# Two layers of spectral mixing and attention: later row aggregation, one product for the values, query halves, middle rows turned by DMA, a new order

## The chip, the cores and the metric

The kernel runs on one core of a Trainium2 chip. The metric is the device time of one execution in microseconds, lower is better. A core has five engines that run their own instruction queues in order and meet at semaphores: TensorE (PE in the profile, with its weight loads as PEld), VectorE (DVE), ScalarE (ACT), GpSimd (POOL) and SyncE (SP), which here only issues DMAs.

## The reference

The input x has 2048 rows of 512 bf16 values. Two pairs of layers follow each other. A mixing layer takes the layer norm of x, its two-dimensional real Fourier transform, multiplies it with a complex weight, transforms back and adds the result to x. An attention layer takes the layer norm of x, makes 32 query heads of 16 columns each with one shared key and value head, and adds the projected result.

```python
def _layernorm(x, axis=-1, eps=1e-5):
    m = jnp.mean(x, axis=axis, keepdims=True)
    v = jnp.var(x, axis=axis, keepdims=True)
    return (x - m) / jnp.sqrt(v + eps)
...
def _A_ref(x, w_r, w_i):
    X = rfft2(x.astype(jnp.float32))
    X = X * (w_r + 1j * w_i)
    return irfft2(X, s=(S, D)).astype(jnp.bfloat16)
...
q, k, v = heads(x @ wq), x @ wk, x @ wv
scores = jnp.einsum("bhqd,bkd->bhqk", q, k) * (Dh ** -0.5)
p = _softmax(scores, axis=-1)
o = jnp.einsum("bhqk,bkd->bhqd", p, v)
return merged(o) @ wo
...
x = x + _A_ref(_layernorm(x), A_w_r, A_w_i)
x = x + _B_ref(_layernorm(x), B_wq, B_wk, B_wv, B_wo)
x = x + _A_ref(_layernorm(x), A_w_r, A_w_i)
x = x + _B_ref(_layernorm(x), B_wq, B_wk, B_wv, B_wo)
```

## The kernel before

The rows stay in on-chip memory as `x_sb`, in four tiles t = 0 to 3 of four row groups r = 0 to 3 with 128 rows each. A layer (a mixing and an attention, class `Layer`) has these stages.

*Front* (`add_stats`, `add_front`). For each tile, VectorE takes `bn_stats` and `bn_aggr` of each row group (`bn`), ScalarE makes the reciprocal deviation with a logarithm and an exponential (`rstd`, which adds the epsilon from a small tensor `eps`), TensorE turns pairs of row groups (`tr_x`) and multiplies them with the Fourier table (`mm1`), ScalarE scales the result (`mm1_evac`), and VectorE combines the four row groups (`radix_g`). In layer 2 the first three tiles are turned by DMA instead: `turn_x` writes a pair of row groups to a DRAM buffer `way` and a DMA transpose reads it back (`turned`).

*Middle* (`add_middle`). TensorE transforms along the rows (`mid`, L1207 to L1209), ScalarE copies, VectorE multiplies with the weight (`filt`, L1233 to L1236).

*Back* (`add_back`). For each tile t the inverse transform (`inv`, L1262), its copies, the radix step on VectorE (`radix_v`), the last product (`y_mm`, L1306), and the sum with x: for t = 0 on TensorE and a ScalarE copy (`put_x`, L1313), otherwise on VectorE (`add_x`, L1317). Then the second layer norm: `bn` (L1091, L1092), `rstd` (L1103, L1104), `shift` (L1108, the negated product of mean and reciprocal deviation) and `apply` (L1115). TensorE turns the normalised rows (`tr_n`, L1323), VectorE or ScalarE copies them (`trn_evac`, L1326), and TensorE makes the keys (`k_mm`, L1340), queries and values (`v_mm`, L1352). `k_evac` (L1346, L1348) writes the keys of even and odd heads to `KA` and `KB`; `v_evac` (L1360, L1362) writes four copies of the values, each with its own factor, since VectorE's approximate exponential is a sum of three phases.

*Attention* (`Attn`). There are 32 blocks: four groups of 512 query rows (qb), four groups of eight heads (g) and two parities of heads (par, which picks `KA` or `KB`). A block has 64 units of 128 keys by 512 queries of one head. A unit goes one of two ways. ScalarE takes two units at once through its exponential (`exp`, L1387). VectorE takes one unit through a multiply-add to 16-bit integers (`p1`, L1394), and two more phases of four units follow, on GpSimd (`phase`, L1398) or VectorE (L1400). TensorE makes the scores (`scores`, L1382) and accumulates the products with the values (`pv`, L1404). When a block is done, `evac` (L1411) transposes it in blocks of 32; after two parities `recip` (L1416), `mul` (L1422) and a turn follow, by DMA (`norm_dma`) or for the last two blocks on VectorE (`norm`, L1431); after four g, `close_rows` projects the rows (`proj`, L1447) and adds them to x. In layer 1 this starts the next layer's front for those rows; in layer 2 each row group is written out (L1453).

The order of all instructions is made ahead of time by a planner (class `Plan`). It keeps a clock for each engine, prices each task, and at each step issues the task that can start first. Background tasks have a priority, an order number and a delay (`lazy`). For a DMA turn it expects a fixed time: `TURN` is 7000 ns and `OUT_TURN` 25000 ns. `fill` puts products of zeros (`dummy`, L1073) into TensorE's queue where it would be idle, which keeps its clock up. VectorE takes units only once the values of all four tiles are there (`dve_on`). A string `SCRIPT` lists steps at which the planner's choice is to be changed: a number of steps, and a kind of change from `TURNS`. `RANKS` is empty and has no effect.

The planner's scores use two PSUM tiles of two banks for ScalarE (`sa`) and four single banks (`b`), which VectorE's scores share with the accumulators and all background products.

Of the kernel before, what the change touches and what calls it, by code (L numbers as in the profile page):

```python
# [10 lines left out]
P = 128  # L11
# [8 lines left out]
R = 4  # L20
# [69 lines left out]
def phase_weights():  # L90
# [4 lines left out]
RANKS = ((), ())  # L95
TURNS = ("PE", "ACT", "DVE", "POOL", "wait", "few", "heads", "phase")
SCRIPT = (
    "0ax00902q00k05h0hw0po0c807l04j03c00801i00a00p0740ay04w00p01v0vn01903p0790l900i01f0630fk00q01202z0ad09i01h07k0h8"
    "08t0ib00a02g04s0bp08300c02q05k05101200q02300s00903n0960b202107m0ac07h00e00e01e0dc03g0by04r0500bx0rl00g0q803f06u"
    "03d03s02t00a01c08001401711p01q05g00j0ex0iy00t01a03807p05t08200k07409503o00g00x00g03914a00804107x04k01m0310ix00s"  # L100
    "02400u0rv02g05707s09a08805q02o03u02206s0mg03l01k02o03u01t00c04w07401m01l01o09s0d90w50ak0240ng09e03407500p00w00c"
    "06o06d08t03h02l0650c81380aq04o04u01h03f00r08i0190dc0bh11p0ud0e404z02103c01l01n02502s05k09906903f01y00x016018083"
    "03h00y02w02l01x06j0hy00o00r0at01q00z00w05n06m0lt05e00c05k0fx0i00740200m40560fx0mh01i00h04402000d00x02j07102x00k"
    "0b201101l0fc04t06q00p01101y0ls00m04w00i05n01x00j00902803m00s03m02u00l01808y0ba0a50z80wa00s0hw08o02c0ml084")


def script():

    out, n = {}, 0
    for i in range(0, len(SCRIPT), 3):  # L110
        v = int(SCRIPT[i:i + 3], 36)
        n += v // 8
        out.setdefault(n, []).append(TURNS[v % 8])
    return out


class Task:
# [5 lines left out]
    def __init__(self, eng, dur, deps, fn, take=None, give=(), then=None, prio=-1, order=0, lazy=0.0, gap=0.0, parts=1, port=False, lock=False, cols=None):  # L123
# [7 lines left out]
        self.end = self.slot = None  # L131


class Plan:
# [34 lines left out]
    OUT_TURN = 25000.0  # L169
# [3 lines left out]
    def __init__(self):  # L173
        self.t = {"PE": 0.0, "ACT": 0.0, "DVE": 0.0, "POOL": 0.0}
# [18 lines left out]
        self.ranks, self.base = None, 0  # L193

    def ranked(self, which):

        self.ranks, self.base = RANKS[which], self.n

    def add(self, *a, **kw):
        k = Task(*a, **kw)  # L200
        k.seq, k.born = self.n, self.t[k.eng]
        self.n += 1
        if self.ranks is not None and k.order < 30:
            i = k.seq - self.base
            if i < len(self.ranks):
                k.prio, k.order, k.lazy = -1, self.ranks[i] / 32, 0.0
        for e in k.ways:
            self.bg[e].append(k)
        return k
# [14 lines left out]
    def step(self):  # L224
        while True:
# [13 lines left out]
            self.turns.discard(eng)  # L239
            return  # L240
# [36 lines left out]
    def bg_next(self, eng):  # L277
        best = None
        for k in self.bg[eng]:
            if any(d.end is None for d in k.deps):  # L280
                continue
            if eng == "ACT" and len(k.ways) > 1 and self.at is not None and self.at.dve_on:
                continue
# [106 lines left out]
    def usable(self, kind):  # L390
# [9 lines left out]
        else:  # L400
            sd, free = (sum(1 for x in self.use if x == y) for y in ("sd", None))
            if not free or sd >= 3 or not at.dve_on and (sd >= self.EARLY_SD or free < 2 or not at.begun or us[0][1] // 4 not in at.v_ready):
                return False
# [3 lines left out]
        return at.unit_ready(us[0]) is not None  # L407

# [87 lines left out]
    def fill(self, start, after):  # L496
# [3 lines left out]
        while self.activity(start) < warm:  # L500
# [8 lines left out]
            else:  # L509
                return  # L510
            if start - t0 < self.MM + (self.PE_SW if mode != after else 0.0) and self.activity(start) >= force:
                return
# [3 lines left out]
            self.t["PE"] = t0 + self.MM  # L516
            if fresh:
                self.bank[i] = t0 + self.MM
# [115 lines left out]
class Attn:  # L634


    def __init__(self, plan, em, layer):
        self.plan, self.em, self.layer = plan, em, layer
        self.blocks = [(qb, g, par) for qb in range(NQB) for g in range(4) for par in range(2)]
        nb = len(self.blocks)  # L640
        first = [(b, 4 * t + r) for t in range(4) for b in range(layer.NFIRST) for r in range(4)]
# [53 lines left out]
    def unit_ready(self, u):  # L695
        b, kc, h = u
        qb, g, par = self.blocks[b]
        if (g, qb) not in self.qt_ready or (kc // 4, par) not in self.k_ready:
            return None
        return max(self.qt_ready[(g, qb)], self.k_ready[(kc // 4, par)])  # L700
# [10 lines left out]
    def done(self, b, slot, end):  # L711
# [5 lines left out]
        self.evac[b] = self.evac_last = ev  # L717
        if par == 0:
            return
        tail = 0.0 if b >= len(self.blocks) - 2 else 5000.0  # L720
        rc = p.add("DVE", 260.0, [ev, self.evac[b - 1]], lambda k: em.recip(self, b), lazy=tail)
        mu = p.add("DVE", 600.0, [rc], lambda k: em.mul(self, b), lazy=tail, port=True)
        if b < len(self.blocks) - 2:
            no = Mark("DMA", None)

            def turned(k):
                em.norm_dma(self, b)
                no.end = k.end + p.OUT_TURN

            mu.then = turned  # L730
        else:
            no = p.add("DVE", 626.0, [mu], lambda k: em.norm(self, b), lazy=tail)
        self.evac[b] = no
        if g == 3:
            self.layer.close_rows(qb, [self.evac[8 * qb + 2 * i + 1] for i in range(4)])


class Layer:
# [9 lines left out]
    PUTC = True  # L748
    FIRST_PUT = (0,)
    BN = ((4,), (4,), (4,), (2, 2))  # L750
    FIRST_EV = ("ACT",)
    FIRST_EV2 = ("ACT",)

    def __init__(self, plan, em, first, last):
# [5 lines left out]
        self.mm1_done = {}  # L760
        self.g_done = {}
# [5 lines left out]
    def pieces(self, durs, deps, fn, order, lazy=0.0, lock=False):  # L767

        for i, d in enumerate(durs):
            deps = [self.plan.add("DVE", d, deps, lambda k, i=i: fn(i), order=order, lazy=lazy, port=True, lock=lock)]  # L770
        return deps[0]


    def add_stats(self, key, tiles, deps):
# [3 lines left out]
        for i, (t, r) in enumerate(tiles):  # L778
            y = getattr(deps[i], "put", None)
            ks.append(p.add("DVE", 795.0, deps[i:i + 1], lambda k, i=i, y=y: em.bn(self, key, i, tiles[i], len(tiles), y and y.slot),  # L780
                            lazy=0.0 if y else 3000.0, order=5))
            if y:
                deps[i].x = p.add("ACT", 482.0, deps[i:i + 1], lambda k, t=t, r=r, y=y: em.put_x(t, r, y.slot), order=1)
                p.both(deps[i].x, ks[-1], y)
        self.add_rstd(key, tiles, ks)

    def add_rstd(self, key, tiles, ks):
        k = self.plan.add("ACT", 450.0, ks, lambda k: self.em.rstd(self, key, len(tiles)), order=5)
# [73 lines left out]
    def add_back(self):  # L862
        p, em, at = self.plan, self.em, self.at
        left = [T]
        for t in range(T):
            o = 20 + 10 * t
            cs = []
            for b in range(2):
# [17 lines left out]
                cs.append(self.pieces((332.0, 332.0, 400.0, 400.0), es, lambda i, t=t, b=b: em.radix_v(self, t, b, i), o))  # L886
            w = 2 if t == 0 else R
            te = []
            for j in range(0, R, w):
                key, ks = ("b", t, j), []  # L890
                for i, r in enumerate(range(j, j + w)):
                    put = t in self.FIRST_PUT
                    n = 5 if put else 4
                    y = p.add("PE", 217.0 * n, cs, lambda k, s, t=t, r=r, n=n: em.y_mm(self, t, r, k.slot, s, n), parts=n, take="b",
                              order=o + 1)
                    if put:
                        c = p.add("ACT", 482.0, [y], lambda k, t=t, r=r, y=y: em.put_x(t, r, y.slot), order=o + 1)
                        b = p.add("DVE", 795.0, [y], lambda k, key=key, i=i, t=t, r=r, w=w, y=y:
                                  em.bn(self, key, i, (t, r), w, y.slot), order=o + 2)
                        p.both(c, b, y)  # L900
# [3 lines left out]
                    ks.append(p.add("DVE", 795.0, [z], lambda k, key=key, i=i, t=t, r=r, w=w: em.bn(self, key, i, (t, r), w),  # L904
                                    order=o + 2))
                rs = p.add("ACT", 450.0, ks, lambda k, key=key, w=w: em.rstd(self, key, w), order=o + 3)
                nb = p.add("DVE", 100.0, [rs], lambda k, key=key, w=w: em.shift(self, key, w), order=o + 3)
                for i, r in enumerate(range(j, j + w)):
                    self.stat[("b", t, r)] = (rs, key, i)
                for a in range(j, j + w, 2):  # L910
                    ap = [p.add("DVE", 323.0, [nb], lambda k, t=t, r=r: em.apply(self, t, r), order=o + 3) for r in (a, a + 1)]
# [24 lines left out]
            p.add("DVE", 524.0, [m], lambda k, t=t, m=m: em.v_evac(t, m.slot), give=(m,), then=v_got, order=o + 6)  # L936
# [5 lines left out]
    def close_rows(self, qb, deps):  # L942
# [595 lines left out]
```

The softmax here doesn't subtract the row's maximum and nothing guards it: scores larger than these inputs give would overflow.

## Time and profile before

| | |
|---|---|
| time, median of 3 runs | 1314.85 us (1314.13 to 1315.22) |
| span of the profiled execution | 1312.7 us |
| granted TensorE clock | 1.00 |
| DMA | 33.04 MB, mean 25 GB/s |

Each stage has its place in the span. Layer 1's front lies before about 23 us, its middle between 22 and 50 us, its back between 50 and 108 us, and its attention runs until 666 us. Layer 2's last tile goes through the front until 682 us, its middle until about 706 us, its back until 760 us, and its attention until 1304 us; the last rows are written after that. In the page's second part each digit is the busy tenth of one of 40 slices of the span:

```profile
DVE  6999999999999999999979999999999999999998
ACT  6488999999999999999954899999999999999996
```

VectorE and ScalarE are full in both attentions; the low digits of ScalarE are the front, middle and back stages of the two layers.

A line of the timeline has the start in us, the duration in us, the engine, the line of the code, the operation, output and inputs, and in brackets the idle time before it with what ended it. Durations overlap a little where an engine starts an instruction before the one ahead has ended, so the step from start to start is the cost.

### The profile page before, as it was taken

What the parts mean: (1) busy time and instruction counts of PE and PEld (TensorE: products, weight loads), DVE (VectorE), ACT (ScalarE), POOL (GpSimd) and SP (SyncE); (2) the same over time, 40 slices, a digit from 0 to 9 for tenths busy, and PEclk for the clock granted to TensorE, in tenths of its full rate; (3) what the DMA queues carried; (4) which work ended last, traced back from release to release, by engine and by line L of the source; (5) the groups of instructions that cost most, each with busy time, mean ns of one, the idle gap of its engine ahead of it and who ended that gap; (6) DMA issues with size and microseconds to landing.
All of it is one profiled execution on the core that took longest, in us unless ns stands there. A gap on an engine that the chain in (4) does not pass through costs nothing.

```text
span 1312.7 us, 31767 instructions
## 1 busy us (share of the span) xinstructions
PE 1281.5 (98%) x12986; PEld 433.1 (33%) x12986; DVE 1272.7 (97%) x2277; ACT 1223.3 (93%) x1397; POOL 840.1 (64%) x825
## 2 busy tenths in 40 slices
PE   9999999999999999999999999999999999999997
PEld 5642222322232222222256423232222232233222
DVE  6999999999999999999979999999999999999998
ACT  6488999999999999999954899999999999999996
POOL 0005777767777677766720067787777777777775
PEclk9999999999999999999999999999999999999999
DMA  9100000011010100010051000000100010000101
GB/s 294 46 1 1 10 9 10 9 32 19 2 12 12 36 10 10 9 34 17 10 169 41 1 1 9 10 10 9 22 14 10 9 22 14 5 8 11 27 5 25
DMA packets 108722, 33.04 MB, mean 25 GB/s; under 512 B 88352, under 2 KB 107296, under 8 KB 108576
## 3 DMA queue, kind: packets, MB, share of 16 engines
q1 hardware_dynamic: 108288, 30.46, 10.0%
q8 instruction: 101, 1.65, 0.5%
q10 hardware_dynamic: 288, 0.56, 0.1%
q14 instruction: 45, 0.37, 0.1%
HBM read 17.89 MB, written 7.60 MB: 19 GB/s over the span
## 4 chain that ended last, share of the span: by engine, by line
ACT 72%; PE 18%; DVE 10%; issue 1%; DVEq 0%
ACT e_0_84 L1387 3%; ACT e_10_94 L1387 3%; ACT e_13_97 L1387 3%; ACT e_3_87 L1387 3%; ACT e_20_104 L1387 3%; ACT e_4_88 L1387 3%; ACT e_12_96 L1387 3%; ACT e_2_86 L1387 3%; ACT e_8_92 L1387 3%; ACT e_7_91 L1387 3%; ACT e_11_95 L1387 3%; ACT e_18_102 L1387 3%; ACT e_1_85 L1387 3%; ACT e_5_89 L1387 3%; ACT e_15_99 L1387 3%; ACT e_14_98 L1387 3%
## 5 line engine op out<-in xcount | busy, mean ns | idle before, releaser
L1382 PEld LDWEIGHTS <-KB 32*128 32x128 bf16 x2048 | 89.7, 91 | 228.5 <-issue 221.4
L1382 PEld LDWEIGHTS <-KA 32*128 32x128 bf16 x2048 | 86.4, 91 | 238.4 <-issue 231.5
L1404 PEld LDWEIGHTS <-vs_116 128*32 128x32 bf16 x2474 | 99.9, 94 | 93.0 <-issue 87.9
L1404 PEld LDWEIGHTS <-vs_117 128*32 128x32 bf16 x1622 | 96.0, 94 | 64.0 <-issue 60.5
L1404 PEld LDWEIGHTS <-vs_118 128*32 128x32 bf16 x1622 | 70.6, 94 | 70.5 <-issue 65.9
L1404 PEld LDWEIGHTS <-vs_119 128*32 128x32 bf16 x1622 | 68.4, 94 | 64.8 <-issue 61.4
L1398 POOL INT64_ADD w_1382<-w_1381 x1 | 1.0, 1040 | 108.1 <-DVE w_1381 L1394 108.1
L1398 POOL INT64_ADD w_10977<-w_10976 x1 | 1.0, 1038 | 97.2 <-DVE w_10976 L1394 97.2
L1387 ACT ACTIVATE e_6_90<-sa_64 128x1024 bf16<-128x1024 f32 x34 | 39.8, 1172 | 1.0 <-PE sa_65 L1382 1.0
L1091 DVE BATCH_NORM_STATS2 st<-x_sb 128x6 f32<-128x512 bf16 x52 | 35.4, 682 | 4.0 <-DMA x_sb<-in_A_x_dram 3.6
L1387 ACT ACTIVATE e_11_95<-sa_65 128x1024 bf16<-128x1024 f32 x31 | 36.5, 1178 | 0.7 <-PE sa_65 L1382 0.7
L1387 ACT ACTIVATE e_12_96<-sa_65 128x1024 bf16<-128x1024 f32 x31 | 36.9, 1189 | 0.2 <-PE sa_65 L1382 0.2
L1387 ACT ACTIVATE e_2_86<-sa_64 128x1024 bf16<-128x1024 f32 x31 | 36.5, 1178 | 0.4 <-PE sa_64 L1382 0.4
L1387 ACT ACTIVATE e_4_88<-sa_65 128x1024 bf16<-128x1024 f32 x31 | 36.6, 1182 | 0.1
L1387 ACT ACTIVATE e_1_85<-sa_64 128x1024 bf16<-128x1024 f32 x31 | 36.6, 1180 | 0.1
L1387 ACT ACTIVATE e_7_91<-sa_64 128x1024 bf16<-128x1024 f32 x31 | 36.6, 1181 | 0.0
L1387 ACT ACTIVATE e_15_99<-sa_65 128x1024 bf16<-128x1024 f32 x31 | 36.6, 1179 | 0.0
L1387 ACT ACTIVATE e_20_104<-sa_65 128x1024 bf16<-128x1024 f32 x31 | 36.4, 1175 | 0.0
L1387 ACT ACTIVATE e_13_97<-sa_64 128x1024 bf16<-128x1024 f32 x31 | 36.2, 1168 | 0.0
L1387 ACT ACTIVATE e_14_98<-sa_65 128x1024 bf16<-128x1024 f32 x31 | 36.0, 1162 | 0.0
L1387 ACT ACTIVATE e_0_84<-sa_65 128x1024 bf16<-128x1024 f32 x30 | 35.5, 1183 | 0.2 <-PE sa_65 L1382 0.2
L1387 ACT ACTIVATE e_9_93<-sa_64 128x1024 bf16<-128x1024 f32 x30 | 35.1, 1170 | 0.2 <-PE sa_64 L1382 0.2
(4077 smaller groups left out, 6474.8 us busy)
## 6 DMA issues: line engine op xcount, KB each, us to landing
it<-const_IT SPq DMA_DIRECT2D x8, 640.0 KB, 5.6
onw<-on SPq DMA_DIRECT2D x120, 32.0 KB, 1.9
x_sb<-in_A_x_dram SPq DMA_DIRECT2D x4, 512.0 KB, 6.8
out_dram<-x_sb SPq DMA_DIRECT2D x16, 128.0 KB, 1.9
way<-x_sb SPq DMA_DIRECT2D x6, 256.0 KB, 2.2
tab_PH<-const_PH ACTq DMA_DIRECT2D x1, 512.0 KB, 4.9
w_131<-const_FT SPq DMA_DIRECT2D x1, 512.0 KB, 8.8
w_136<-const_FT SPq DMA_DIRECT2D x1, 512.0 KB, 8.4
```

The lines of the kernel that those rows point to most:

```text
L1091: self.nc.vector.bn_stats(st, self.ps(slot) if slot else self.x[:, x[1], x[0], :])
L1382: self.nc.tensor.matmul(o, lhsT=KX[rs, kc * P:(kc + 1) * P], rhs=at.QT[qb][rs, g, :], start=True, stop=True, skip_group_check=True)
L1387: self.wrote("ACT", e, self.nc.scalar.activation(out=e, in_=self.ps(slot), func=ACT.Exp, scale=SCALE))
L1398: self.nc.gpsimd.int64_add(t[p][:, 0:n].bitcast(U64), t[0][:, 0:n].bitcast(U64), DELTA[p] * FOUR)
L1404: self.nc.tensor.matmul(self.ps(slot)[32 * h:32 * h + 32, :], lhsT=V[:, kc, :], rhs=rhs, start=first, stop=last, skip_group_check=True)
```

## The change

The parts are these.

- `bn` aggregates a row group's statistics when those of the next one have been taken; the last call of a group aggregates what is left. The planner's price goes from 795 ns each to 585, 685 or 800 ns.
- `rstd` takes the epsilon as an immediate number. `shift` is gone: `apply` subtracts the mean and multiplies by the reciprocal deviation.
- `v_evac` writes all four value copies with one VectorE product; the factors stand in a small tensor `vw` that GpSimd fills.
- The normalised rows of tiles 1 and 2 are turned by DMA (`turn_n`: two writes of one row group each and a transpose of both), not by TensorE and a copy.
- In the back, `y_mm` of a row group waits only for the radix piece that makes it, and row groups go in the order 0, 2, 1, 3 for tiles 0 and 3.
- The last two blocks of a layer (`halves`) no longer take one parity of heads with 512 queries but both parities with 256 queries each. Each of their scores is two products of 256 columns. `recip`, `mul`, `norm` and `close_rows` follow after each of them, for two row groups.
- The first tile of x is loaded in two halves, arrival times and the price of zero products before 4400 ns are changed, `OUT_TURN` is 9000 ns.
- `TURNS` has a ninth kind, `flex` (ScalarE may take a copy that VectorE could take too, also during full attention); VectorE's scores leave a bank free when an urgent product of `close_rows` needs it; `SCRIPT` is new.

```diff
-TURNS = ("PE", "ACT", "DVE", "POOL", "wait", "few", "heads", "phase")
+TURNS = ("PE", "ACT", "DVE", "POOL", "wait", "few", "heads", "phase", "flex")
...
-    OUT_TURN = 25000.0
+    COLD = 4400.0
+    OUT_TURN = 9000.0
...
-        self.t = {"PE": 0.0, "ACT": 0.0, "DVE": 0.0, "POOL": 0.0}
+        self.t = {"PE": 1200.0, "ACT": 0.0, "DVE": 0.0, "POOL": 0.0}
...
-            if not free or sd >= 3 or not at.dve_on and ...
+            if not free or sd >= 3 or free < 2 and self.pressed() or not at.dve_on and ...
...
-            self.t["PE"] = t0 + self.MM
+            end = self.t["PE"] = t0 + (self.MM if t0 > self.COLD else 430.0)
...
+        self.halves = {nb - 2: 0, nb - 1: 1}
...
+        if b in self.halves:
+            rc = p.add("DVE", 125.0, [ev], lambda k: em.recip(self, b))
+            mu = p.add("DVE", 335.0, [rc], lambda k: em.mul(self, b), port=True)
+            no = p.add("DVE", 340.0, [mu], lambda k: em.norm(self, b))
+            hf = self.halves[b]
+            self.layer.close_rows(qb, [self.evac[8 * qb + 2 * i + 1] for i in range(3)] + [no], (2 * hf, 2 * hf + 1))
+            return
...
+    DMA_T = (1, 2)
+    RSTD = 357.0
+    BN_T = (585.0, 685.0, 800.0)
...
-                rs = p.add("ACT", 450.0, ks, lambda k, key=key, w=w: em.rstd(self, key, w), order=o + 3)
-                nb = p.add("DVE", 100.0, [rs], lambda k, key=key, w=w: em.shift(self, key, w), order=o + 3)
+                rs = p.add("ACT", self.RSTD, ks, lambda k, key=key, w=w: em.rstd(self, key, w), order=o + 3)
...
+                    if d == 1:
+                        te.append(Mark("DMA", None))
+
+                        def applied(k, t=t, a=a, y=te[-1], ap=ap):
+                            if all(z.end is not None for z in ap):
+                                em.turn_n(self, t, a)
+                                y.end = k.end + p.TURN
+                        ap[0].then = ap[1].then = applied
+                        continue
...
     def bn(self, L, key, i, x, n, slot=None):
-        st = self.small([6], "st")
-        self.nc.vector.bn_stats(st, self.ps(slot) if slot else self.x[:, x[1], x[0], :])
-        self.nc.vector.bn_aggr(mv[:, i, :], st)
+        late = L.bn_late[key]
+        late.append((i, self.small([6], "st", 8)))
+        self.nc.vector.bn_stats(late[-1][1], self.ps(slot) if slot else self.x[:, x[1], x[0], :])
+        L.bn_left[key] = L.bn_left.get(key, n) - 1
+        for j, st in late[:] if L.bn_left[key] == 0 else late[:-1]:
+            self.nc.vector.bn_aggr(L.sb[key][0][:, j, :], st)
+            late.pop(0)
...
-        self.nc.vector.tensor_scalar(out=xn, in0=self.x[:, r, t, :], scalar1=sb[:, 0, i:i + 1], scalar2=sb[:, 1, i:i + 1],
-                                     op0=ALU.mult, op1=ALU.add)
+        self.nc.vector.tensor_scalar(out=xn, in0=self.x[:, r, t, :], scalar1=mv[:, i, 0:1], scalar2=sb[:, 0, i:i + 1],
+                                     op0=ALU.subtract, op1=ALU.mult)
...
+    def turn_n(self, L, t, a):
+
+        if t not in L.at.xT:
+            L.at.xT[t] = self.t4([NC, R, P], tag="gx", bufs=4)
+        way = self.way.tile([2 * P, D], BF, name="way", tag="way")
+        for i in range(2):
+            self.nc.sync.dma_start(out=way[P * i:P * i + P, :], in_=L.xn.pop((t, a + i)))
+        out = L.at.xT[t].rearrange("p c r x -> p c (r x)")[:, :, P * a:P * a + 2 * P]
+        self.nc.sync.dma_start_transpose(out=out, in_=way)
...
-        for i, v in enumerate(self.VS):
-            dst = v[:, 4 * t:4 * t + 4, 0:DH]
-            if i == 0:
-                self.nc.vector.tensor_copy(out=dst, in_=src)
-            else:
-                self.nc.vector.tensor_single_scalar(out=dst, in_=src, scalar=self.pw[i - 1], op=ALU.mult)
+        shape = [P, 1 + K_PH, R, DH]
+        self.nc.vector.tensor_tensor(out=self.vs[:, :, 4 * t:4 * t + 4, 0:DH], in0=src.unsqueeze(1).to_broadcast(shape),
+                                     in1=self.vw.to_broadcast(shape), op=ALU.mult)
...
+            if b in at.halves:
+                q = 256 * at.halves[b]
+                for i, KX in enumerate((self.KA, self.KB)):
+                    self.nc.tensor.matmul(o[:, 256 * i:256 * i + 256], lhsT=KX[rs, kc * P:(kc + 1) * P],
+                                          rhs=at.QT[qb][rs, g, q:q + 256], start=True, stop=True, skip_group_check=True)
+                continue
...
-        arrive = Mark("DMA", 5500.0 + 2600.0 * t)
+        arrive = [Mark("DMA", x) for x in ((3800.0, 3800.0, 4600.0, 4600.0) if t == 0 else (5200.0 + 2000.0 * t,) * R)]
```

## The prediction

> **What bounds the kernel now.** I read the page's totals first, then a table of busy time in stretches of 20 us, then the VectorE and TensorE timelines of the stages that the change touches, and last the waits of SP's DMA queue.
>
> The totals, and stretches of the start of layer 1 (its attention begins in earnest near 108 us), one steady stretch and the change of layers (columns: TensorE, weight loads, VectorE, ScalarE, GpSimd busy us with instruction counts, clock, DMA share, GB/s):
>
> ```profile
> PE 1281.5 (98%) x12986; PEld 433.1 (33%) x12986; DVE 1272.7 (97%) x2277; ACT 1223.3 (93%) x1397; POOL 840.1 (64%) x825
> ```
> ```profile
> 72.00:108.00 36.00, 34.05 (x301) 15.62 (x300) 32.54 (x93) 29.68 (x39) 0.00 (x0) 1.00 0.00 1
> 780.00:1280.00 500.00, 493.98 (x5290) 147.29 (x5288) 498.51 (x835) 500.00 (x547) 389.67 (x376) 1.00 0.07 12
> ```
> ```profile
> 660.00:680.00 20.00, 18.99 (x144) 9.21 (x141) 13.17 (x25) 11.47 (x19) 4.10 (x4) 1.00 0.83 260
> ```
>
> In steady attention ScalarE is busy 500.00 of 500 us and VectorE 498.51: both take score units from one pool, so only less work on one of them shortens it. One ScalarE exp covers two units in 0.917 us (the step in the chain of waits, 1285.66 to 1286.58), 2.18 units/us; VectorE starts a first-phase product every 0.60 us, 1.67 units/us. Together 3.85. Hence my exchange rate: 1 us of VectorE work removed there is worth 1.67/3.85 = 0.43 us of time, 1 us of ScalarE work 0.57 us.
>
> The stages before attention (44 to 108 us and 684 to 760 us) are a VectorE chain; ScalarE already runs exps there (29.68 of 36 us busy). The change of layers is a latency chain: VectorE 13.17, ScalarE 11.47 of 20 us.
>
> Row statistics and value copies, from VectorE's timeline of the first of these stages:
>
> ```profile
> 87.39 0.69 DVE L1091 BATCH_NORM_STATS2 st<-x_sb 128x6 f32<-128x512 bf16 x1
> 88.11 0.18 DVE L1092 BATCH_NORM_AGGREGATE mv<-st 128x2 f32<-128x6 f32 x1
> 88.20 0.66 DVE L1091 BATCH_NORM_STATS2 st<-x_sb 128x6 f32<-128x512 bf16 x1
> ...
> 94.86 0.21 DVE L1360 CAST vs_116<-b_66 128x64 bf16<-128x64 f32 x1
> 94.99 0.22 DVE L1362 TENSOR_SCALAR vs_117<-b_66 128x64 bf16<-128x64 f32 x1
> 95.12 0.22 DVE L1362 TENSOR_SCALAR vs_118<-b_66 128x64 bf16<-128x64 f32 x1
> 95.25 0.22 DVE L1362 TENSOR_SCALAR vs_119<-b_66 128x64 bf16<-128x64 f32 x1
> 95.46 0.69 DVE L1317 TENSOR_TENSOR x_sb<-b_68,x_sb 128x512 bf16<-128x512 f32 x1
> ```
>
> A tile's statistics cost 88.20 - 87.39 = 0.81 us, of which the aggregation starts only 0.72 after its source began: it waits for it. Four value copies take 95.46 - 94.86 = 0.60 us.
>
> The start, TensorE's timeline:
>
> ```profile
> 6.80 0.38 PE L1073 MATMUL b_66<-zero 128*128 128x512 bf16 x1
> 7.01 0.61 PE L1152 MATMUL b_67<-tab_ident,x_sb 128*128 128x128 bf16 x8
> ```
> ```profile
> 4.77 0.69 DVE L1091 BATCH_NORM_STATS2 st<-x_sb 128x6 f32<-128x512 bf16 x1 [3.62 <-DMA x_sb<-in_A_x_dram]
> ```
>
> VectorE has its first rows at 4.77; TensorE is still working off warm-up products and turns them only at 7.01. The first ten of these took 0.43 us each, not the 0.22 the planner counts.
>
> A DMA-turned pair of rows, from SP's queue (layer 1's attention) and the page's DMA issues:
>
> ```profile
> 279.19 0.39 SPq L1133 DMA_DIRECT2D way<-x_sb  x1
> 281.43 1.27 SPq L1126 DMA_TRANSPOSE e_17_101<-way  x1
> ```
> ```profile
> e_17_101<-way SPq DMA_TRANSPOSE x1, 3.2
> ```
>
> Write issued at 279.19, turn at 281.43, landed 3.2 later: 5.4 us, and SP stands still between write and turn.
>
> And the last lines of the end:
>
> ```profile
> 1303.88 0.72 DVE L1411 STREAM_TRANSPOSE raw<-b_66 128x512 f32<-128x512 f32 x1 [0.91 <-PE b_66 L1404]
> 1308.75 0.68 DVE L1317 TENSOR_TENSOR x_sb<-b_66,x_sb 128x512 bf16<-128x512 f32 x1
> ```
>
> **What the Trainium skill says.** "TensorE: Matmul & The Clock Gate", part 1, gives start-to-start 426.7 ns at N = 512 cold and 215.7 warm; the trace agrees (0.43, 0.22). "ScalarE: Activation LUTs", "What ACT_TABLE_LOAD costs": each pointer operand adds about 93 ns to an ACTIVATE; the trace fits (the epsilon-reading Ln 0.30 us, the Exp behind it 0.20). "DMA: Bandwidth & Descriptors", "Anatomy of one DMA": about 2.0 us of a transfer is fixed, mostly completion, measured on another issuing path; here the write to the turn takes 2.24. "VectorE: DVE Perf Modes", "The DRAIN you can't avoid": minimise the number of operations, and a same-engine read after write needs a semaphore or an operation between. The 0.72 agrees.
>
> **The change, part by part.** Minus is saved.
>
> *Start.* The first tile's load is split in two, warm-up products are priced cold, rows expected at 3.8 us. Turning can begin near 4.3 rather than 7.01, its ScalarE copy (1.0 us) ends near 6.2; the phase table, issued at 1.19 and 4.9 us in flight, lands at 6.1. So mm1 begins near 6.4 instead of 8.73: -2.3. SP carries one more issue (about 0.5 us) before the weight loads; those are needed only from 22 us, and TensorE's later chain to 43.5 has no DMA wait. Bounds: 0 (the table or ScalarE ends last) to -2.7.
>
> *Statistics, shift, values, in each back stage.* An aggregation put one tile later no longer waits: 0.81 becomes about 0.60 for the stats' own step plus 0.10 for the small one. A group of four saves 0.42, of two 0.2 (its last aggregation still waits). Per stage three fours and two twos: 1.7 us. Five shifts (0.1 to 0.17) go: 0.6. Values: 0.60 becomes one operation over 256 elements; no row shows it, bounds 0.25 and 0.55, I take 0.36: 4 x 0.24 = 1.0. Middle rows: tr_n's evacuations for tiles 1 and 2 go, three on VectorE (0.60) and one on ScalarE (0.9), with four TensorE turns of about 0.5 us. VectorE total 1.7 + 0.6 + 1.0 + 1.8 = 5.1; some 0.8 of it lies in tile 0, before the first exp (72 and 723 us), and counts in full. The other 4.3: a stage shortened by d loses ScalarE exps, which fill 82% of it, so d is worth d(1 - 0.57 x 0.82) = 0.53d: 2.3. ScalarE's 0.9 gives 0.5. Per stage -3.6, minus 0.3 because TensorE (34.05 of 36 us) does not always deliver sooner: -3.3, two stages -6.6. Bounds: -3 (all at 0.43, half hidden) to -11 (all in full). The immediate epsilon saves 0.09 x 20 on a mostly waiting ScalarE: 0. Layer 2's early statistics within attention, three fours: 1.27 x 0.43 = -0.5.
>
> *Middle rows' lateness.* A turn on TensorE takes about 1.3 us with its copy. turn_n issues two writes (0.8), waits about 1.85, issues the turn (1.27), which lands 3.2 after its issue; the second pair's writes stand behind the first turn in SP. So the second pair is there some 0.8 + 1.85 + 1.27 + 0.8 + 1.85 + 3.2 = 9.8 us after the first pair's rows, about 9 after its own; the planner counts 7.0. k_mm stands in TensorE's order where it was planned, and scores, y_mm and inverse products queue behind it; VectorE and ScalarE wait for those. Four such tiles, 0.5 us each on average, since the plan rarely places k_mm at its first moment: +2. Bounds 0 to +9. The SP loads of the inverse tables are issued at the first inv of the tile before and wait for a buffer freed earlier; I cost them at nothing. Attention needs the middle keys only after tile 0's sixteen units per head group, and tile 3 still takes TensorE's way, so the last V is not delayed.
>
> *Query halves for the last two blocks.* Change of layers: last accumulation 666.1, radix_g at 679.24, 13.1 us. With two rows left: evac 0.72, reciprocal, product and turn of half size 0.95, projection 0.9, two statistics and copies to about 4.8, turn and copy 6.2, two mm1 8.0, copy 8.8: -4.3. But the first half's 2.9 us VectorE (normalising, two statistics, an evacuation) and 2.5 us ScalarE now lie in saturated attention: 2.9 x 0.43 + 2.5 x 0.57 = +2.7, and two rows holding PSUM banks starve VectorE's scores a little, +0.5. Net -1.1. Bounds -3.5 to +2. End: 1303.88 to 1309.35 is 5.5 us; with halves about 3.4: -2.1, against 2.05 us VectorE moved forward, +0.9: -1.2. Each score of these blocks becomes two 256-column products with two weight loads, on a TensorE with little room: +0.5, bounds 0 to +3.
>
> *New order* of the searched script, and the flex turns: both engines are full before, so 0, with +-3. The shorter expected output turn and the one delay for all normalisations move VectorE work about inside full attention, and GpSimd's four more small fills come before its first phase at 108 us: 0.
>
> Sum: -2.3 - 6.6 - 0.5 + 2 - 1.1 - 1.2 + 0.5 = -9.2. The profiled span is 1312.7; 1303.5 after. The runs' median lies 2.1 above the span (1314.85), so 1305.6.
>
> **Rivals.** *Slower: late turns stall TensorE.* Place: k_mm of tiles 1 and 2. If the second turn lands 9 us after its rows where 7 were planned and k_mm stands at its planned moment, each stall is 2 to 4 us with DVE and ACT buffers run dry. Four at 3 are 12, and the later middle keys idle ScalarE by about 3 us a stage (3.4 in time): -11.2 + 12 + 3.4 = +4, 1319. It decides from about 2.8 us a tile. For: the in-order queues and the sum of 9.8. Against: a 7-us allowance and the slack of the plan. *Little change:* ScalarE and TensorE bound the back stage as much as VectorE (29.7 and 34.05 of 36 us), and the halves cost what they give: start -2.3 and 1 us elsewhere, 1311.5. *More:* VectorE's savings in the back stages count in full (5.1 + 0.9 each instead of 3.3) and turns are hidden: -9.2 - 5.4 - 2, about 1298. That the change does not do what it says is excluded for the removed operations, not for their being late.
>
> **How the numbers follow.** About 0.2% (2.6 us) can be told from no change. Forecast case, 1301 to 1311: 0.62. More: 0.12. Little change: 0.13, half of it within 0.2%. Slower: 0.13. Faster 0.62 + 0.12 + 0.06 = 0.80, same 0.07, slower 0.13. The range 1297 to 1316 takes in the larger gain, little change and a part of the slower case.
>
> **What would show it.** Right: the first turning product near 4.5 us; statistics at 0.70 a tile; one VectorE operation per value tile; radix_g of layer 2 about 9 us after the last accumulation; an end of 3.5 us after it. Wrong: TensorE waits above 2 us at k_mm on the DMA turn; ScalarE idle between tiles' keys; VectorE below 99% before the last block ends.

## The result, and the profile after

| | before | after |
|---|---|---|
| median of 4 runs each | 1314.70 us (1314.13 to 1315.22) | 1318.84 us (1317.94 to 1321.58) |
| ratio, with its 95% interval | | 1.0035 (1.0018 to 1.0052) |
| span of the profiled execution | 1312.7 us | 1319.8 us |
| granted TensorE clock, mean | 1.00 | 0.991 |

The kernel became slower by about 4 us, where 9 us less were predicted. The forecast was wrong; the rival "late turns stall TensorE" named the mechanism, and its 1319 lies beside the measured time by luck (below). The profiled execution after is the slowest of its four (1321.58) and has the lowest mean clock (0.991, the others 0.994 to 0.996), so times along its profile lie some 3 us above those of a median run.

The page's totals and the clock by slices:

```profile
PE 1283.0 (97%) x13187; PEld 434.4 (33%) x13187; DVE 1265.3 (96%) x2247; ACT 1223.1 (93%) x1397; POOL 836.0 (63%) x822
PEclk9997999999999999999999999999999999999999
```

VectorE did get 7.4 us less work (1272.7 before). It didn't help: the span grew, so the idle time of the full engines grew. The 7 in the clock's fourth slice (99 to 132 us) is new. The stretches say where (columns as in the prediction: TensorE, weight loads, VectorE, ScalarE, GpSimd, clock, DMA share, GB/s):

```profile
72.00:108.00 36.00, 31.25 (x230) 13.57 (x229) 26.25 (x68) 22.39 (x31) 0.00 (x0) 0.85 0.26 59
780.00:1280.00 500.00, 495.09 (x5289) 149.34 (x5286) 497.41 (x832) 499.67 (x546) 386.11 (x372) 1.00 0.07 12
660.00:680.00 20.00, 19.21 (x218) 8.75 (x215) 17.05 (x33) 14.85 (x23) 7.17 (x7) 1.00 0.74 221
740.00:760.00 20.00, 16.11 (x129) 5.52 (x130) 12.04 (x33) 12.29 (x18) 0.00 (x0) 0.83 0.22 53
```

Steady attention is as full as before. The back stages are not: from 72 to 108 us VectorE went from 32.54 to 26.25 busy us, ScalarE from 29.68 to 22.39 (39 instructions to 31), at a clock of 0.85. In layer 2 the same stage (740 to 760) shows VectorE at 12.04 of 20, at a clock of 0.83; before, these 20 us were:

```profile
740.00:760.00 20.00, 17.64 (x166) 7.41 (x159) 17.05 (x47) 16.06 (x21) 0.00 (x0) 1.00 0.00 1
```

The line from 660 to 680 is not the same stage in both kernels: layer 1's attention ends at 666.2 before and at 673.1 after. TensorE's waits in the back stages, from its timeline (in brackets the idle time and what ended it; `gx` holds the turned rows, `wk` the weights of the keys):

```profile
84.53 1.04 PE L1396 MATMUL b_67<-gx,wk_81 128*128 128x512 bf16 x4 [1.76 <-DMA gx<-way]
...
97.05 1.46 PE L1396 MATMUL b_67<-gx,wk_81 128*128 128x512 bf16 x4 [1.89 <-DMA gx<-way]
...
740.12 1.02 PE L1396 MATMUL b_66<-gx,wk_81 128*128 128x512 bf16 x4 [2.08 <-DMA gx<-way]
...
753.29 1.86 PE L1396 MATMUL b_66<-gx,wk_81 128*128 128x512 bf16 x4 [2.59 <-DMA gx<-way]
```

These are `k_mm` of tiles 1 and 2 in both layers: all four that read DMA-turned rows wait, 8.3 us together. What SP's queue (SPq) did ahead of the second one (`xnt` are the normalised rows, `way` the DRAM buffer):

```profile
86.71 1.18 SPq L1188 DMA_DIRECT2D way<-xnt  x2
89.31 1.23 SPq L1190 DMA_TRANSPOSE gx<-way  x1
90.60 1.46 SPq L1188 DMA_DIRECT2D way<-xnt  x2
93.71 1.23 SPq L1190 DMA_TRANSPOSE gx<-way  x1
```

The second pair's writes start 3.9 us after the first pair's, behind its turn. The turn is issued at 93.71 and its rows are there when `k_mm` begins, at 97.05: 10.3 us after the first write (9.5 us for tile 1's, from 75.00 to 84.5).

### The profile page after: what moved, and what is told of

Read it like the earlier page. It is cut to its first block, busy times and chain, and to the rows that moved or that the text cites. A ratio compares the mean times of both kernels' runs of the same rounds, so it can differ in the third digit from the quotient of the medians.

```text
span 1319.8 us, 32181 instructions
## 1 busy us (share of the span) xinstructions
PE 1283.0 (97%) x13187; PEld 434.4 (33%) x13187; DVE 1265.3 (96%) x2247; ACT 1223.1 (93%) x1397; POOL 836.0 (63%) x822
## 3 DMA queue, kind: packets, MB, share of 16 engines
q1 hardware_dynamic: 119056, 34.66, 11.2%
## 4 chain that ended last, share of the span: by engine, by line
ACT 69%; PE 21%; DVE 6%; DMA 2%; issue 1%; SPq 0%; DVEq 0%; ACTq 0%
ACT e_4_88 L1447 3%; ACT e_12_96 L1447 3%; ACT e_10_94 L1447 3%; ACT e_5_89 L1447 3%; ACT e_0_84 L1447 3%; ACT e_3_87 L1447 3%; ACT e_19_103 L1447 3%; ACT e_9_93 L1447 3%; ACT e_20_104 L1447 3%; ACT e_2_86 L1447 3%; ACT e_1_85 L1447 3%; ACT e_7_91 L1447 3%; ACT e_11_95 L1447 3%; ACT e_16_100 L1447 3%; ACT e_15_99 L1447 3%; ACT e_14_98 L1447 3%
## 5 line engine op out<-in xcount | busy, mean ns | idle before, releaser
L1464 PEld LDWEIGHTS <-vs 128*32 128x32 bf16 x7340 | 140.2, 94 | 280.7 <-issue 262.7
L1442 PEld LDWEIGHTS <-KA 32*128 32x128 bf16 x1920 | 82.2, 91 | 227.7 <-issue 221.6
L1442 PEld LDWEIGHTS <-KB 32*128 32x128 bf16 x1920 | 84.7, 91 | 216.4 <-issue 209.3
L1447 ACT ACTIVATE e_19_103<-sa_64 128x1024 bf16<-128x1024 f32 x32 | 36.8, 1148 | 0.6 <-PE sa_64 L1442 0.3
L1447 ACT ACTIVATE e_6_90<-sa_64 128x1024 bf16<-128x1024 f32 x31 | 36.1, 1166 | 1.0 <-PE sa_65 L1442 1.0
L1447 ACT ACTIVATE e_14_98<-sa_65 128x1024 bf16<-128x1024 f32 x32 | 36.3, 1136 | 0.5 <-PE sa_65 L1442 0.5
L1447 ACT ACTIVATE e_7_91<-sa_64 128x1024 bf16<-128x1024 f32 x31 | 35.4, 1142 | 1.0 <-PE sa_64 L1442 1.0
L1447 ACT ACTIVATE e_11_95<-sa_65 128x1024 bf16<-128x1024 f32 x31 | 36.3, 1172 | 0.0
L1447 ACT ACTIVATE e_9_93<-sa_64 128x1024 bf16<-128x1024 f32 x31 | 35.9, 1157 | 0.3 <-PE sa_64 L1442 0.3
L1447 ACT ACTIVATE e_5_89<-sa_65 128x1024 bf16<-128x1024 f32 x31 | 36.1, 1165 | 0.0
L1447 ACT ACTIVATE e_10_94<-sa_64 128x1024 bf16<-128x1024 f32 x31 | 36.1, 1164 | 0.0
L1447 ACT ACTIVATE e_3_87<-sa_64 128x1024 bf16<-128x1024 f32 x29 | 33.6, 1160 | 2.2 <-PE b_67 L1442 2.1
L1447 ACT ACTIVATE e_3_87<-sa_65 128x1024 bf16<-128x1024 f32 x30 | 34.9, 1165 | 0.6 <-PE sa_65 L1442 0.6
L1447 ACT ACTIVATE e_20_104<-sa_65 128x1024 bf16<-128x1024 f32 x30 | 34.8, 1160 | 0.8 <-PE sa_64 L1442 0.8
L1447 ACT ACTIVATE e_12_96<-sa_64 128x1024 bf16<-128x1024 f32 x30 | 35.2, 1173 | 0.2 <-PE b_69 L1442 0.2
L1447 ACT ACTIVATE e_15_99<-sa_65 128x1024 bf16<-128x1024 f32 x30 | 35.0, 1167 | 0.3 <-PE sa_65 L1442 0.3
L1447 ACT ACTIVATE e_4_88<-sa_65 128x1024 bf16<-128x1024 f32 x30 | 35.0, 1168 | 0.0
L1447 ACT ACTIVATE e_2_86<-sa_65 128x1024 bf16<-128x1024 f32 x30 | 34.7, 1157 | 0.3 <-PE b_67 L1442 0.3
L1447 ACT ACTIVATE e_16_100<-sa_64 128x1024 bf16<-128x1024 f32 x30 | 34.9, 1164 | 0.0
```

The lines of the kernel that those rows point to most:

```text
L1442: self.nc.tensor.matmul(o, lhsT=KX[rs, kc * P:(kc + 1) * P], rhs=at.QT[qb][rs, g, :], start=True, stop=True, skip_group_check=True)
L1447: self.wrote("ACT", e, self.nc.scalar.activation(out=e, in_=self.ps(slot), func=ACT.Exp, scale=SCALE))
L1464: self.nc.tensor.matmul(self.ps(slot)[32 * h:32 * h + 32, :], lhsT=V[:, kc, :], rhs=rhs, start=first, stop=last, skip_group_check=True)
```

## Experiments

Times are medians; a ratio is that to the kernel before on the same chip, with its 95% interval. Kernels 1 to 4 ran together (before: 1314.66), 5 to 8 (1314.33) and 9 to 12 (1314.54).

**1. Keys and values that don't wait for the turn.** The turns, queues and order stay; the products read other rows (shown are the changed parts of two lines).

```diff
-rhs=self.xTc(L.at, t, c)
+rhs=self.xTc(L.at, 0 if t in L.DMA_T else t, c)
...
-lhsT=L.at.xT[t][:, c, r, :]
+lhsT=L.at.xT[0 if t in L.DMA_T else t][:, c, r, :]
```

> Keys and values of tiles 1 and 2 are made from tile 0's turned rows, so that nothing in the back stage waits for the DMA turns, which are still issued; every queue has the same instructions in the same order. It leaves out the right keys and values of those tiles. Theory (late turns stall TensorE at k_mm, and its clock then falls to half): no wait at k_mm, clock 1.00 throughout, 1303 to 1308 us, 11 to 16 us under the changed kernel. Rival (halves and new order cost the time): above 1314 us.

1307.69 us (1306.20 to 1308.56), ratio 0.9945 (0.9932 to 0.9959): 11.2 us less than after. The same windows of its profile:

```profile
72.00:108.00 36.00, 33.30 (x275) 14.46 (x276) 30.03 (x76) 27.16 (x37) 0.00 (x0) 0.96 0.28 60
```

TensorE issues 275 matmuls in the stretch where after issues 230. The DMA traffic is unchanged, so it is the wait for the turned rows that makes the kernel slower than before, and not the traffic of the turns, the doubled scores or the new order. The clock is 0.96 in this stretch and not 1.00 throughout, as was expected; it falls here without such a wait (last section).

**2. The writes of the turn on GpSimd's queue.** The same work, but the second pair's writes no longer stand behind the first pair's turn.

```diff
-            self.nc.sync.dma_start(out=way[P * i:P * i + P, :], in_=L.xn.pop((t, a + i)))
+            self.nc.gpsimd.dma_start(out=way[P * i:P * i + P, :], in_=L.xn.pop((t, a + i)))
```

> The two writes of each turn of tiles 1 and 2 are issued by GpSimd, which is idle then, so that the second pair's writes no longer stand behind the first pair's turn in SP's queue; all other queues are unchanged. Theory: the second turn is issued about 2.5 us earlier, which takes the wait at k_mm (2.4 to 2.9 us) to under 1 us: 1304 to 1309 us. If the transfers themselves are the delay and not the order in SP's queue: waits of 2 us remain and 1315 to 1320 us.

1309.29 us (1307.56 to 1310.05), ratio 0.9958 (0.9946 to 0.9971): 9.5 us less than after, and 5.4 less than before; a little above the range that was expected. GpSimd's writes, from its timeline, and the wait that is left at the second `k_mm`, from TensorE's:

```profile
85.66 2.25 POOL L1188 DMA_DIRECT2D way<-xnt  x4 [7.99 <-DVE xnt L1159]
```
```profile
94.09 1.04 PE L1396 MATMUL b<-gx,wk 128*128 128x512 bf16 x4 [0.24 <-DMA gx<-way]
```

All four writes go within 2.25 us, and the rows are there 8.4 us after the first (10.3 after the change as made). A write from this queue lands no sooner (2.1 us, 1.9 from SP), so what was gained is the place in the queue. GpSimd does nothing else at that time. This kernel computes the whole of the reference and beats both.

**3. TensorE kept busy in the wait.** Eleven products of zeros ahead of each such `k_mm`, to part the wait from the lower clock that follows it.

```diff
     def k_mm(self, L, t, slot, c):
+        if c == 0 and t in L.DMA_T:
+            for _ in range(11):
+                self.dummy(slot[1], True, "full")
```

> Eleven products of zeros (2.4 us warm) are put ahead of k_mm of tiles 1 and 2, into the bank that k_mm then overwrites: the wait stays, TensorE is busy through it. If the clock that falls after the wait is the larger part of the cost: clock 1.00 and 1309 to 1313 us. If the wait itself is the larger part: 1316 to 1320 us.

1317.17 us (1315.49 to 1320.50), ratio 1.0020 (1.0014 to 1.0027): 1.7 us less than after, with intervals that overlap.

```profile
72.00:108.00 36.00, 33.44 (x260) 15.33 (x263) 27.49 (x71) 24.24 (x34) 0.00 (x0) 1.00 0.25 59
```

The clock is back at 1.00, yet VectorE and ScalarE are hardly busier up to 108 us. The low clock lasts longer than this stretch; from 100 to 120 us, after and here:

```profile
100.00:120.00 20.00, 20.00 (x150) 5.91 (x146) 12.51 (x24) 14.84 (x17) 2.41 (x2) 0.64 0.00 1
```
```profile
100.00:120.00 20.00, 18.53 (x195) 6.24 (x195) 16.86 (x31) 18.69 (x22) 4.47 (x4) 1.00 0.01 2
```

There both engines are some 4 us busier. But these are the slowest run of the one kernel and the fastest of the other, 6 us apart; by the medians 1.7 us come back of 11.2. So the larger part of the cost is the wait itself, during which the scores behind `k_mm` don't come. The clock's part is near 2 us: small, and by these intervals not told apart from zero. The zeros end up to 0.5 us after the rows have landed (85.02 at tile 1 of layer 1), so they hide a little of it.

**4. The planner told the truth about the turn.**

```diff
-                                y.end = k.end + p.TURN
+                                y.end = k.end + 10000.0
```

> The planner expects 10 us for a turn of tiles 1 and 2 where it expected 7. Everything after that is planned anew, and the script's steps then meet other choices. Theory: no wait at k_mm over 1 us, clock 1.00, and 1305 to 1313 us, the higher the more the script was worth. Rival (halves and order): above 1316 us.

1345.16 us (1342.39 to 1349.67), ratio 1.0236 (1.0218 to 1.0255). This missed what every theory gave. The searched script holds choices by step number; with another due time the steps shift and the choices fall on other instructions. TensorE's waits for turned rows at `k_mm` are down to 1.3 us in all, 0.9 at most, as the theory had it, but losses show far from there: from 1280 to 1300 us VectorE is busy for 14.92 of 20 us, at a clock of 0.66. So the run says nothing of what the wait costs; it shows that this planner's price can't be changed under this script without a new search.

**5. One product for a score.** On kernel 2; in `scores`, `if b in at.halves:` becomes `if False:`.

> On top of the kernel with the writes issued by GpSimd (1309.3 us): each score of the last two blocks is one product of 512 columns again, with one key table; it leaves out the other parity of heads and half the queries there. Nothing else moves. The prediction priced the doubled products and weight loads at 0.5 us, bounds 0 and 3: 1306.3 to 1309.3 us expected, 1308.8 most likely. If doubled scores starve the exponentials: under 1306 us.

1308.05 us (1306.75 to 1309.79), ratio 0.9953 (0.9940 to 0.9965): 1.2 us below kernel 2, the intervals overlap. The doubled scores cost between nothing and some 2 us.

**6. The small VectorE edits alone**, in before's order.

```diff
...
-        self.nc.vector.bn_aggr(mv[:, i, :], st)
+        for j, st in late[:] if L.bn_left[key] == 0 else late[:-1]:
+            self.nc.vector.bn_aggr(L.sb[key][0][:, j, :], st)
...
-        for i, v in enumerate(self.VS):
...
+        self.nc.vector.tensor_tensor(out=self.vs[:, :, 4 * t:4 * t + 4, 0:DH], in0=src.unsqueeze(1).to_broadcast(shape),
+                                     in1=self.vw.to_broadcast(shape), op=ALU.mult)
```

> The kernel before in its own order, with only late aggregation, no shift, immediate epsilon and one value product. By the prediction's terms: 3.3 us of VectorE work in each back stage, 0.5 of it in full and the rest at 0.53, so 2.0 us a stage, and 0.5 us for layer 2's early statistics: 1310.2 us, bounds 1307.5 (all in full) and 1311 (all at 0.43). If TensorE or the fixed order sets the pace of the back stages: 1313.5 to 1314.7 us.

1309.64 us (1308.92 to 1310.27), ratio 0.9961 (0.9948 to 0.9975): 4.7 us less than before. These parts work, and do so without a new order.

**7. The start alone**, in before's order: the first tile in two loads, 11 of the zero products left out.

```diff
+        if 6 < self.zeros <= 17:
+            return
...
-        for t in range(T):
+        for j in (0, 2):
+            self.nc.sync.dma_start(out=self.x[:, j:j + 2, 0], in_=self.xv[:, j:j + 2, 0])
+        for t in range(1, T):
```

> The kernel before in its own order, with the first tile loaded in two halves and eleven of the first seventeen products of zeros left away. By the prediction's first term the first Fourier product starts 2.3 us earlier, and all that follows: 1312.4 us. If DMA arrivals or ScalarE set the front's end: 1314 to 1315 us.

1313.09 us (1312.77 to 1316.43), ratio 0.9995 (0.9987 to 1.0004): 1.2 us less by the medians, not told apart from no change. The first turn begins at 4.32, but the second pair's rows come late:

```profile
6.41 0.62 PE L1157 MATMUL b<-tab_ident,x_sb 128*128 128x128 bf16 x8 [1.10 <-DMA x_sb<-in_A_x_dram]
```

Its first `mm1` starts at 7.30 (before 8.73), and the 1.4 us gained there agree with 1.2 of time.

**8. No halves at the end.** On kernel 2; layer 2's last two blocks as before.

```diff
-        self.halves = {nb - 2: 0, nb - 1: 1}
+        self.halves = {} if layer.last else {nb - 2: 0, nb - 1: 1}
...
```

> On top of the kernel with the writes issued by GpSimd (1309.3 us): the last two blocks of layer 2 alone take one parity of heads with all queries again, and the four row groups are closed after the last. By the prediction's term for the end (-2.1 of latency, +0.9 of work moved forward) this is 1.2 us slower: 1310.5 us. If the halves cost attention what they give: 1309 us. If their doubled scores and held banks cost more: under 1308 us.

1309.65 us (1308.19 to 1311.52), ratio 0.9961 (0.9949 to 0.9974): kernel 2's time within 0.4 us. The halves at the end gain nothing that shows.

**9. Kernels 6 and 7 in one.**

> The kernel before in its own order, with the small VectorE parts (1309.6 us alone) and the earlier start (1313.1 us alone) together. If both lie on one chain they add up: 1308.4 us. If the earlier start is lost behind VectorE: 1309.5 us.

1308.26 us (1308.09 to 1309.44), ratio 0.9953 (0.9941 to 0.9966): the two parts add up. This kernel too beats both; it isn't told apart from kernel 2, and needs neither the turns nor the halves nor another order.

**10 and 11. No script**, in before and in kernel 2 (`SCRIPT = ""`).

> The kernel before with an empty script: the planner's own choices everywhere. This shows what the script is worth. Prediction's view (engines full, order worth under 3 us): 1314 to 1318 us. If the script carries most of the packing, as the replanned kernel at 1345 us suggests: 1325 us and more.

> The changed kernel with the turns' writes issued by GpSimd and an empty script. Against the kernel before with an empty script it shows the parts of the change without a searched order. If the parts are worth what they are in the searched order, about 5 us less than that kernel; if the changed parts need their script, as much or more.

1332.63 us (1332.54 to 1332.73), ratio 1.0137 (1.0122 to 1.0153), and 1332.68 us (1330.34 to 1336.04), ratio 1.0140 (1.0125 to 1.0154). The searched order is worth 18 us in before and 23 us in kernel 2. Without it the two are equal: the parts of the change then bring nothing that shows. Why that is so was not settled.

**12. No halves at the change of layers.** On kernel 2, with layer 1's last two blocks as before; of this run only the stretch up to layer 2's first filter is read, as the order after it is no longer the searched one (the single run took 1320.28 us).

> On top of the kernel with the writes issued by GpSimd: the last two blocks of layer 1 alone take one parity with all queries again, statistics in pairs. What follows in layer 2 is planned anew, so only the stretch up to layer 2's first full filter product is read. Prediction (latency -4.3, work moved forward +2.7, banks +0.5 with halves): last accumulation 3 us earlier (663.5 us instead of 666.5), first filter product 20 us after it instead of 16.9, at 684.5 instead of 683.4 us. If halves gain nothing: at 683.4 or before.

The last accumulation, and then the first `radix_g` of layer 2, in this kernel and in kernel 2:

```profile
665.71 0.72 DVE L1481 STREAM_TRANSPOSE raw<-b 128x512 f32<-128x512 f32 x1 [0.50 <-PE b L1470]
...
678.48 0.69 DVE L66 TENSOR_TENSOR w<-w 128x1024 bf16<-128x1024 bf16 x1 [3.48 <-ACT w L1237]
```
```profile
666.53 0.72 DVE L1473 STREAM_TRANSPOSE raw<-b 128x512 f32<-128x512 f32 x1 [0.55 <-PE b L1464]
...
676.53 0.69 DVE L66 TENSOR_TENSOR w<-w 128x1024 bf16<-128x1024 bf16 x1 [3.53 <-ACT w L1231]
```

The chain is 12.8 us without the halves and 10.0 with them, against 0.8 us that attention ends later. By the first filter (685.40 against 683.40) 2.0 us are left. Each side is one trace; kernel 12's is 0.4 us ahead already at 633 us, long before the last two blocks, so 2.4 may be nearer.

## Why the prediction was wrong, point by point

**The step that failed** is the size put on the middle rows' lateness: "0.5 us each on average, since the plan rarely places k_mm at its first moment: +2". Taking the wait away (kernel 1) gives back 11.2 us, and taking two writes out from behind a turn (kernel 2) 9.5: 2.4 to 2.8 us for each of the four tiles, not 0.5. The working ahead of that number was right. It had the second pair at "9.8 us after the first pair's rows, about 9 after its own" and the planner at 7.0 for the latter. The trace shows 9.5 and 10.3 from the first write (layer 1), and 8.6 to 9.1 after the pair's own rows were normalised (tile 2 of layer 1: VectorE ends at 86.93 + 1.05 = 87.98, shown below, and `k_mm` begins at 97.05). So the rows came 1.6 to 2.1 us late, and TensorE waited 1.76 to 2.59 us for them: the lateness became a stall in full, in all four places. What failed was the reason for the 0.5, that a plan leaves slack; this order, made for a turn of 7.0 us, had none at `k_mm`. Two of the waits are above the 2 us that the prediction named as a sign of being wrong, and even its bound of +9 was a little low.

The rival had the mechanism right. It asked for 3 us a tile on TensorE and another 3.4 us for later keys, 15.4 in all; TensorE shows 8.3 of waits, and kernel 1 gives back 11.2. Its -11.2 for everything else was too good by the same 4.2 us (kernel 1 is 7.0 below before), so that its sum came out at 1319 is luck. The 2.9 us between 8.3 and 11.2 are near what keeping the clock up gave (1.7, kernel 3). The profile's account of the waits at `k_mm`, in the kernel after:

```profile
its engine sat idle before it (us, times) until:
  DMA gx<-way: 13.0, 6
...
who waited for it (us, times):
  ACT KA L1402: 12.1, 5
  DVE KA L1404: 5.4, 3
```

The 13.0 counts TensorE and its weight loads both. In kernel 2 the same row reads 1.8 us, 3 times, and in kernel 1 ScalarE and VectorE wait 3.9 and 2.4 us for `k_mm`.

**Start, -2.3.** The size was about half: -1.2 by the medians (kernel 7, not told apart from nothing alone; kernel 9 is 1.6 better than kernel 6, each against its own before). The first turn began at 4.40 as forecast, the first `mm1` at 6.89 and not 6.4, as the second half tile of x landed only at 6.4.

**Statistics and values, part of -6.6.** The new durations came as forecast. VectorE's timeline after:

```profile
86.59 0.42 DVE L1414 TENSOR_TENSOR vs<-b_68,vw 128x256 bf16<-128x256 f32 x1
86.93 1.05 DVE L1159 TENSOR_SCALAR xnt<-x_sb,mv,sb 128x512 bf16<-128x512 bf16 x3
...
94.29 0.69 DVE L1137 BATCH_NORM_STATS2 st<-x_sb 128x6 f32<-128x512 bf16 x1
94.90 0.17 DVE L1140 BATCH_NORM_AGGREGATE mv<-st 128x2 f32<-128x6 f32 x1
94.98 0.66 DVE L1373 TENSOR_TENSOR x_sb<-b_68,x_sb 128x512 bf16<-128x512 f32 x1
```

A row group's statistics step is 94.98 - 94.29 = 0.69 (0.70 forecast, 0.81 before), with the aggregation no longer waiting. The value product's step is 86.93 - 86.59 = 0.34 (0.36 forecast). Of the 6.6, the removed TensorE turns were 2.9 by the prediction's own prices (1.8 us of VectorE at 0.53 and 0.5 for ScalarE, twice), and the small edits the remaining 3.7, with 0.5 more in layer 2's attention. Kernel 6 measured 4.7 for these 4.2. One reading behind the rate of 0.53 was off: ScalarE's 29.68 busy us of 36 were taken for exps, but its 25 exps are 24.0 of them, the rest copies and small operations. With 0.67 for 0.82 the rate is 1 - 0.57 x 0.67 = 0.62, and the 4.2 become 4.6.

**Halves.** At the change of layers -1.1 was forecast and -2.0 to -2.4 seen (kernel 12, with the doubled scores in it): radix_g comes 10.0 us after the last accumulation, not 13.1. At the end -1.2 was forecast. The tail is short as said:

```profile
1313.34 0.72 DVE L1473 STREAM_TRANSPOSE raw<-b_66 128x512 f32<-128x512 f32 x1
...
1316.37 0.68 DVE L1373 TENSOR_TENSOR x_sb<-b_69,x_sb 128x512 bf16<-128x512 f32 x1
```

It ends 3.7 us after the last accumulation (3.5 forecast, 5.5 before), but without it the kernel is slower by 0.4 us only, which is no difference (kernel 8). The work moved forward into full attention and the doubled scores may have taken the gain back; they were not measured apart there. The doubled scores of both layers (+0.5) cost between nothing and some 2 (kernel 5).

**What is still missing.** Without its lateness the change was forecast at -11.2, and kernel 1 gives -7.0. Of these 4.2 us the start explains 1.1. The small edits gave 0.5 more than forecast, and the halves, forecast at -1.8 with their doubled scores, about -2.4 or more (0.4 and 2.0, kernels 8 and 12). So some 4 us lie with what no run takes apart: the removed turns of the middle rows (-2.9), the new order (0) and the smaller changes that come with it. Put the other way, kernel 9 (-6.3) and the halves (-2.4) make more than the -7.0 of kernel 1, so the turns and the new order together gave nothing there, with runs that tell some 2 us. The reason for the 0, that both engines are full before, did not hold: kernel 10 has the parts of before in another order, and is 18 us slower. Two possible reasons are not shown to be the cause: VectorE joins attention after only 22 ScalarE exps in kernels 1 and 2, where it is 25 in before, while the split of score units between the engines is the same; and in the traces of both the clock falls near 105 us (last section).

**The cold clock** was not in the sum. After the waits TensorE ran at a clock of 0.50 (below), but keeping it up gave only about 1.7 us. The changed kernel's own runs point the same way: the one with a mean clock of 0.991 took 1321.58 us, the three at 0.994 to 0.996 took 1317.94 to 1319.10.

## What to carry to other kernels

When a step is moved to a DMA, follow every instruction in the issuing queue to the arrival of its last part, and compare that with the due time that the order was made for: what comes later becomes a stall where a full in-order engine reaches it, unless slack is shown in the trace of that order. A write and a turn that waits for it don't belong in one queue with the next pair's writes; another queue that is idle at that time took 9.5 us off here. In an order searched choice by choice, a due time could not be corrected afterwards (kernel 4, 26 us slower than after); mending the data's arrival worked (kernel 2), and searching again was not tried.

## What the hardware showed unexpectedly

TensorE's clock fell after a short wait and stayed low for long. The Trainium skill, "TensorE: Matmul & The Clock Gate", part 1, puts the return to full clock at a busy window of about 3.4 us. The windows around and after the wait that ended at 97.05, in the kernel after:

```profile
96.00:98.00 2.00, 0.95 (x4) 0.44 (x5) 0.59 (x3) 0.00 (x0) 0.00 (x0) 0.88 0.21 42
...
102.00:104.00 2.00, 2.00 (x13) 0.98 (x12) 0.76 (x2) 1.02 (x1) 0.00 (x0) 0.50 0.00 0
...
112.00:114.00 2.00, 2.00 (x23) 0.33 (x19) 0.42 (x1) 0.46 (x1) 0.00 (x0) 0.50 0.00 0
```

The clock is 0.54 on the mean from 98 to 116 us, though TensorE is counted busy for 2.00 of 2 us in the last two windows; from 116 to 124 us it is 1.00. The records of the clock in the traces give the length of every low stretch: 17.07 us here and 6.83 us after the wait that ended at 753.29, 3.41 us in kernels 1, 2, 11 and 12, and 3.41, 3.41 and 13.65 us in kernel 4. All are whole multiples of 3.41 us (5, 2, 1 and 4), so the step agrees with the page's window. But five such windows in a row pass here, most of them with TensorE busy by the profile's count: that count doesn't tell when the clock comes back.

The wait alone doesn't tell when it falls either. The clock stays at 1.00 after the waits that ended at 84.53 and 740.12, and in kernels 1 and 2 it falls near 105 us, where no DMA-turned row is waited for. In kernel 3, where products of zeros filled the waits, it doesn't fall. What such a stretch costs can be read once: kernel 8 has the instructions of kernel 2 up to layer 2's last blocks, but in its trace the clock stays at 1.00, and layer 1's last accumulation comes 1.8 us earlier (664.72 against 666.53), about half of the 3.41. What starts and what ends a low stretch the runs don't show.
